# Block-sparse attention and MLP on one core: engine orders made anew, and three of four first summary spreads moved to GpSimd

## The chip, the cores and the metric

One Trainium2 chip, one of its cores. The metric is the device time of one execution in microseconds, the median of three runs, lower is better. Times in the profile count from the first instruction of the profiled execution.

## The reference

```python
def _attn_ref(q, k, v):                      # (4, 8, 768, 64) each, float32
    block, window = (32, 16)
    k_sum = k.reshape(B, H, nb, block, D).max(axis=3)
    v_sum = v.reshape(B, H, nb, block, D).mean(axis=3)
    scores_l = scale * np.matmul(q, k.transpose(0, 1, 3, 2))       # masked to |i - j| < 16
    scores_s = scale * np.einsum('bhsd,bhnd->bhsn', q, k_sum) + np.log(block)
    a = softmax(concat([scores_l masked, scores_s]))               # 768 + 24 columns
    return a @ concat([v, v_sum])

def _moe_ref(x, w_in, w_out):                # x: 3072 x 512, w_in: 512 x 2048, w_out: 2048 x 512
    h = x @ w_in
    g = h * erf(softplus(h))
    return g @ w_out
```

So every token attends to 31 neighbours and to 24 block summaries of its sequence (the maximum of 32 keys, the mean of 32 values), and the result goes through a two-layer MLP.

## The kernel before, in words

The 3072 tokens are cut into 6 chunks of 512. Attention is done by **quads**: a pair of heads (of 4 pairs) in one chunk, so 24 quads; quads 0 to 3 make chunk 0. A quad's scores (`scores`, L580) are matmuls of 64 queries by 96 neighbouring keys and by 24 key summaries. `softmax` (L617) takes the row maximum on VectorE (`red`), the exponentials on ScalarE (`exps`, eight per quad) and scales the rows by their sums on VectorE (`norm`). `transp` (L678) turns the probabilities on TensorE, ScalarE copies the two halves out of PSUM (`ptr`), `av` (L720) multiplies them with the values, and `xsplit` (L741) stores the result as a high and a low float32r part: the high part copied by ScalarE, the low part subtracted by VectorE (line 751). A float32 product is then three float32r matmuls. The MLP goes in 24 periods k = 0 to 23 (6 chunks by 4 groups of 512 hidden columns): `mm1` (L830) is the first layer, `mm2` (L1001) the second, with softplus and erf on ScalarE and the splitting of the hidden values on VectorE between them.

Weights come from HBM as 64-bit numbers. `convert` (L340) packs each of 16 units into float32 with three VectorE operations (L354, L357, L360), then ScalarE makes the high and VectorE the low part (L376). `w0` to `w3` below are the first four units; the products of quads 0 and 1 with group 0 need w0, those of quads 2 and 3 need w1.

The head of the program is special: quads 0 to 3 have their own loads (`load_qk_first`, `load_v_first`, `load_vw_first`). `ksum_first` (L523) makes a quad's key summaries with one VectorE maximum. `vsum_first` (L526) makes all value summaries with 12 slow float32 matmul passes, ScalarE copies them to SBUF (L534), and then each quad's 24 summary rows must be spread into rows 96 to 119 of that quad's value tile `vwf`, eight times side by side (24 x 1024 numbers): `rows_` (L536). Quad p's `av` waits for that (`vwg{p}`). In the kernel before ScalarE spreads three quads' rows and one quad's go by a DMA on SP.

Nothing is issued in the order of the code. Every operation is entered in a `Plan` (L59) with the engines that can do it and assumed durations; `Plan.order` (L104) then simulates the engines and takes, wherever one comes free, the ready operation with the smallest key. The key is a due time worked back from TensorE's order, plus an offset from the table `TUNE` (one entry per operation: offset, penalty for a change of ScalarE's table, which table, which engine). `first_dma` (L294) enters the first loads with assumed transfer times and an assumed landing. TensorE may take operations up to 60 ahead among the first 330, 8 ahead after that. Where the plan sees TensorE idle early, it puts filler matmuls (`busy`, L1047; line 1050 in the profile), at most one per 0.43 us of planned idle time.

Each DMA on SP also waits, in order, for the eighth before it to have landed; every engine executes its own list in order.

Of the kernel before, what the change touches and what calls it, by code (L numbers as in the profile page):

```python
# [23 lines left out]
NP = H // 2  # L24
# [3 lines left out]
NI = NB // 2  # L28
NT = T // 128
NS = 24  # L30
LW = 96
# [27 lines left out]
class Plan:  # L59
# [44 lines left out]
    def order(self, free, window, tune, table):  # L104
# [87 lines left out]
def block_attention_mlp(ctx: ExitStack, tc: tile.TileContext, q_t, k_nat, k_win, v_tok, v_nat, v_win, w_in, w_out, out):  # L192
# [101 lines left out]
    def first_dma(us, fn, r=(), w=(), **kw):  # L294
        return P.add({"SP": us}, lambda e: fn(), r, w, hold=2.0, land=-1.0, **kw)
# [31 lines left out]
    def load_w(u):  # L327
        kind, g, r = u
        n = raw_slot(u)

        def go():
            rw = raws[u] = slot(n, [128, 2, 512, 2], U32, "rw")
            src = (w_in[2 * g + r] if kind == "i" else w_out[2 * g + r]).bitcast(U32).rearrange("p c (f t) -> p c f t", t=2)
            nc.sync.dma_start(out=rw, in_=src)
        if u in units[:4]:
            first_dma(2.6, go, w=[f"w{n}"])
        else:
            dma(1112, go, w=[f"w{n}"])
# [169 lines left out]
    def load_qk_first(p):  # L508
        st[p] = dict(qb=qfs[:, p], vw=vws[p // 2][:, p % 2])
        first_dma(2.7 if p == 1 else 0.97, lambda: nc.sync.dma_start(out=kfirst[p], in_=k_nat[0, p]), w=[f"kf{p}"])  # L510
        first_dma(0.66, lambda: nc.sync.dma_start(out=qfs[:, p], in_=q_t[0, p]), w=[f"qf{p}"])

    def load_v_first():
        for n in range(2):
            def go(n=n):
                for t in range(3):
                    nc.sync.dma_start(out=vts[n][:, t], in_=v_tok[3 * n + t])
            first_dma(2.1 + 0.15 * n, go, w=[f"vt{n}"])

    def load_vw_first(p):  # L520
        first_dma(1.35, lambda: nc.sync.dma_start(out=st[p]["vw"], in_=v_win[0, p]), w=[f"vwf{p}"])
# [43 lines left out]
    def load_quad_v(qd):  # L565
# [12 lines left out]
    PA = ("pA", "pB")  # L578

    def scores(qd, banks=PA):  # L580

# [726 lines left out]
```

## Time and profile before

| | |
|---|---|
| time, median of 3 runs (lowest, highest) | 600.12 us (599.73, 600.18) |
| the profiled execution's own time | 599.8 us |
| its span, first to last instruction | 598.0 us |
| PE (TensorE) busy | 590.6 us, 99% |
| DVE (VectorE) busy | 476.4 us, 80% |
| ACT (ScalarE) busy, of it 98 table loads | 424.3 us, 125.7 us |
| POOL (GpSimd) busy | 4.0 us, all in the first 8 us |
| DMA moved | 169.93 MB, mean 284 GB/s |

Busy time counts an engine as busy also with filler matmuls, and a matmul's end is modelled, so 99% does not say that nothing is lost. The queue that issues DMAs is SP. In the profile PE is TensorE, DVE VectorE, ACT ScalarE, POOL GpSimd.

### The profile page before, as it was taken

The numbers are of one execution on the slowest core, as the hardware profiler recorded it, in microseconds if no ns is written. First come the engines' busy times: TensorE is split into PE (matmuls) and PEld (weight loads), VectorE is DVE, ScalarE is ACT, GpSimd is POOL, SyncE is SP. The second block draws the span as 40 slices with busy tenths as digits, with TensorE's granted clock in tenths as the row PEclk, the third lists the DMA queues.
The fourth block names the chain that finished last, engine by engine and source line by source line (L and its number), as shares of the span: only waits on it lengthen the run. The fifth ranks groups of instructions, "written<-read, shape, count | busy, mean of one in ns | idle before, by whom it ended". The sixth has DMA issues, their size and how long they took to land.

```text
span 598.0 us, 11682 instructions
## 1 busy us (share of the span) xinstructions
PE 590.6 (99%) x4495; PEld 486.1 (81%) x4495; DVE 476.4 (80%) x1001; ACT 424.3 (71%) x824; POOL 4.0 (1%) x30
## 2 busy tenths in 40 slices
PE   8899999999999999999999999999999999999997
PEld 4675666878888889989888888888888888888885
DVE  5999999888999987866989769669778677556553
ACT  6989879989879794674885964846646654852570
POOL 2000000000000000000000000000000000000000
PEclk9999999999999999999999999999999999999999
DMA  8999777668997989899998888787897864774621
GB/s 330 358 418 344 282 253 284 221 247 316 318 344 245 345 323 338 290 351 370 313 376 315 323 310 323 267 302 269 292 304 263 309 226 146 252 243 178 237 72 70
DMA packets 47586, 169.93 MB, mean 284 GB/s; under 512 B 4460, under 2 KB 16940, under 8 KB 34988
## 3 DMA queue, kind: packets, MB, share of 16 engines
q1 hardware_dynamic: 47388, 169.07, 78.1%
q8 instruction: 35, 0.57, 0.4%
q14 instruction: 19, 0.16, 0.1%
q10 hardware_dynamic: 144, 0.13, 0.1%
HBM read 135.66 MB, written 31.46 MB: 279 GB/s over the span
## 4 chain that ended last, share of the span: by engine, by line
PE 96%; ACT 1%; DVE 1%; issue 0%
PE ops L1013 41%; PE h L839 15%; PE ha L891 12%; PE hb L885 7%; PE ops L1009 5%; PE hb L891 4%; PE hb L882 4%; PE pA L600 3%; PE px L735 3%; PE px L732 1%; DVE stats L639 1%; PE pA L687 1%; PE idle L1050 1%; ACT prf L647 0%; PE pB L600 0%; ACT ptr L692 0%
## 5 line engine op out<-in xcount | busy, mean ns | idle before, releaser
L1013 PE MATMUL ops<-w,gh 128*128 128x512 f32 x704 | 230.1, 393 | 0.0
L1013 PEld LDWEIGHTS ops<-w,gh 128*128 128x128 f32 x704 | 132.3, 188 | 27.8 <-issue 0.9
L1013 PE MATMUL ops<-w,gl 128*128 128x512 f32 x352 | 137.5, 391 | 0.0
L1264 ACT ACT_TABLE_LOAD x98 | 125.7, 1283 | 1.7
L839 PE MATMUL h<-x,w 128*128 128x512 f32 x384 | 97.0, 402 | 0.0
L298 ACT COPY hc<-hb 128x256 f32<-128x256 f32 x65 | 23.9, 373 | 102.9 <-PE hb L882 57.0
L839 PEld LDWEIGHTS h<-x,w 128*128 128x128 f32 x384 | 71.1, 188 | 18.5 <-issue 3.6
L1013 PEld LDWEIGHTS ops<-w,gl 128*128 128x128 f32 x352 | 66.2, 188 | 11.8
L989 DVE TENSOR_TENSOR hc<-wt,hc 128x1024 f32<-128x1024 f32 x44 | 53.0, 1219 | 10.7 <-ACT wt L977 10.7
L647 ACT ACTIVATE prx<-prx,stats 128x120 f32<-128x120 f32 x160 | 61.0, 384 | 0.2
L996 DVE TENSOR_TENSOR gl<-hc,gh 128x1024 fp32r<-128x1024 f32 x44 | 53.6, 1220 | 1.0 <-ACT gh L298 0.2
L930 DVE TENSOR_TENSOR hc<-hb,hc 128x256 f32<-128x256 f32 x96 | 38.7, 418 | 15.8 <-ACT hc L298 14.6
L977 ACT ACTIVATE wt<-wt 128x1024 f32<-128x1024 f32 x48 | 50.1, 1058 | 0.4
L965 ACT ACTIVATE wt<-hc 128x1024 f32<-128x1024 f32 x32 | 33.0, 1055 | 8.2 <-DVE hc L930 8.0
L298 DVE CAST gh<-hc 128x1024 fp32r<-128x1024 f32 x37 | 25.5, 690 | 10.6 <-PE ops L1013 9.5
L885 PE MATMUL hb<-w,ws 128*128 128x512 f32 x96 | 30.2, 396 | 0.0
L647 ACT ACTIVATION_READ_ACCUMULATOR prx<-prx,stats 128x1 f32 x160 | 30.0, 187 | 0.0
L1009 PE MATMUL ops<-a32s,gw 128*128 128x512 f32 x64 | 29.6, 597 | 0.0
L633 DVE CUSTOM_DVE_ANT_0 prx<-pA,mask_sb 128x120 f32<-128x120 f32 x64 | 14.2, 278 | 17.7 <-PE pB L600 17.4
L298 DVE COPY hc<-hb 128x256 f32<-128x256 f32 x31 | 13.0, 418 | 18.0 <-PE hb L882 13.8
L891 PE MATMUL ha<-w,ws 128*128 128x256 f32 x192 | 27.2, 283 | 0.0
L891 PE MATMUL ha<-x,w 128*128 128x256 f32 x192 | 27.1, 282 | 0.0
(172 smaller groups left out, 959.8 us busy)
## 6 DMA issues: line engine op xcount, KB each, us to landing
w<-dr SPq DMA_DIRECT2D x36, 1024.0 KB
ws<-ds SPq DMA_DIRECT2D x30, 1024.0 KB
vw<-v_win SPq DMA_DIRECT2D x20, 512.0 KB
kw<-k_win SPq DMA_DIRECT2D x20, 480.0 KB
rw<-w_in SPq DMA_DIRECT2D x8, 1024.0 KB
rw<-w_out SPq DMA_DIRECT2D x8, 1024.0 KB
dr<-w SPq DMA_DIRECT2D x8, 1024.0 KB
dt<-ot SPq DMA_DIRECT2D x16, 512.0 KB
```

What stands on the lines that cost most here:

```text
L298: e.copy(o, i) if e is nc.scalar else e.tensor_copy(o, i)
L647: nc.scalar.activation(s["pr"][:, j], s["pr"][:, j] if qd >= MQ else s["sc"][j // NI][:, i * NK:(i + 1) * NK], AF.Exp, scale=-1.0 if qd >= ...
L839: nc.tensor.matmul(hs[k, f][:, 0:T], lhsT=w[m], rhs=xt[ch, cc][:, x], start=(cc == 0 and n == 0), stop=(cc == 3 and n == 2))
L885: nc.tensor.matmul(full, lhsT=w[0], rhs=y, start=first and c == 0, stop=c == 1, skip_group_check=True)
L891: nc.tensor.matmul(half, lhsT=w[m], rhs=y[:, l], start=first and c == 0 and i == 0, stop=c == 1 and i == 2, skip_group_check=True)
L930: on({"DVE": 0.43}, lambda e: e.tensor_tensor(hc[k, n][:, m, z], bank(n, "b")[:, R], hc[k, n][:, m, z], op=ALU.add), [pair_banks(n)[1]], [ ...
L977: act(0.96, lambda n=n: nc.scalar.activation(wt[k, n], wt[k, n], AF.Erf, scale=-1.0 if k < SOFT else 1.0), [s], [s], table=("sig",), after ...
L989: e.tensor_tensor(hc[k, n], wt.pop((k, n)), hc[k, n], op=ALU.mult)
L996: e.tensor_tensor(gs[k, n][1], hc.pop((k, n)), f32(gs[k, n][0]), op=ALU.subtract)
L1009: nc.tensor.matmul(os_[ch, t], lhsT=x[0][:, i % 2, t * 128:(t + 1) * 128], rhs=w32["o", g, i // 2][:, i % 2], start=first, stop=last)
L1013: nc.tensor.matmul(os_[ch, t], lhsT=x[y][:, i % 2, t * 128:(t + 1) * 128], rhs=w[m], start=first and n == 0, stop=last and n == 2)
L1264: nc.scalar.preload_act_table_set(sets[o["load"]])
```

## The change

`TUNE` is another table (one line of some 60,000 characters, of which only the start stands here), so the order on every engine is new from the first microseconds on. The assumed times of the first loads are changed, and eight of them get fixed places at the head of SP's list (`first`). The spreading of the summary rows may now be done by GpSimd, ScalarE or VectorE instead of ScalarE, VectorE or a DMA; the plan gives quad 0 to ScalarE and quads 1, 2 and 3 to GpSimd. Two further ways (`OWN`, `ASKED`) are in the code with empty lists, so nothing takes them.

```diff
-TUNE = {0: (-400.0, 1.5, 0, None), 1: (-300.0, 1.5, 0, None), 2: (-100.0, 1.5, 0, None), ...
+TUNE = {0: (1.06317, 1.5, 0, None), 1: (0.7965079, 1.5, 0, None), 2: (0.01488405, 1.5, 0, None), ...
...
-            key[n] = later + (n if "PE" in o["eng"] else o["due"])
+            key[n] = later + (n if "PE" in o["eng"] else o.get("first", o["due"]))
...
-        return P.add({"SP": us}, lambda e: fn(), r, w, hold=2.0, land=-1.0, **kw)
+        return P.add({"SP": us}, lambda e: fn(), r, w, hold=2.0, land=-0.9, **kw)
...
-        def summed():
-            nc.scalar.copy(vsum[LW:NK], tiles[bank][LW:NK].rearrange("s (p c) -> s p c", p=NP))
-        act(0.5, summed, [bank], [f"vsum0{p}" for p in range(NP)])
-        def rows_(e, p):
+        on({"ACT": 0.55, "DVE": 0.6}, lambda e: copy(e, vsum[LW:NK], tiles[bank][LW:NK].rearrange("s (p c) -> s p c", p=NP)), [bank], [f"vsum0{p}" for p in range(NP)])
+        def rows_(e, p, ask=False):
             o, i = st[p]["vw"][LW:NK], vsum[LW:NK, p:p + 1, :].to_broadcast([NS, NB, 128])
-            e.dma_start(out=o, in_=i) if e is nc.sync else copy(e, o, i)
+            e.dma_start(out=o, in_=i) if ask or e is nc.sync else copy(e, o, i)
         for p in range(NP):
-            on({"ACT": 0.95, "SP": 0.45} if p else {"DVE": 1.13, "ACT": 0.95}, lambda e, p=p: rows_(e, p), [f"vsum0{p}", f"vwf{p}"], [f"vwg{p}"])
+            ...
+                on(VWG, lambda e, p=p: rows_(e, p), [f"vsum0{p}", f"vwf{p}"], [f"vwg{p}"])
...
+    VWG = {"POOL": 1.6, "ACT": 0.95, "DVE": 1.13}
...
+    for n, p in enumerate((0, 1, 3, 2, 8, 4, 5, 9)):
+        P.ops[p]["first"] = n - 1e6
```

In total the instructions are the same but for these: 9 ScalarE table loads fewer (89 for 98 behind the first), one filler matmul fewer (12 for 13), the spreading as said (one copy on ScalarE for three, three on GpSimd for none, no DMA of `vsum` on SP), and some 10 small copies that go to the other of VectorE and ScalarE.

**VectorE, the first 10 us.** `kf_124` holds the keys of quads 0 and 1; `pA`, `pB` are the two halves of quad 0's scores, `h0`, `h1` those of quad 1. Before:

```order
L524 TENSOR_REDUCE ksum_112<-kf_124 128x24
L639 TENSOR_REDUCE stats_110<-pA_146 128x4
L641 TENSOR_SCALAR stats_110<-stats_110 128x4
L639 TENSOR_REDUCE stats_110<-pB_147 128x4
L641 TENSOR_SCALAR stats_110<-stats_110 128x4
L524 TENSOR_REDUCE ksum_112<-kf_124 128x24
L639 TENSOR_REDUCE stats_110<-h0_195 128x4
```

and now:

```order
L524 TENSOR_REDUCE ksum_112<-kf_124 128x24
L645 TENSOR_REDUCE stats_110<-pA_146 128x4
L647 TENSOR_SCALAR stats_110<-stats_110 128x4
L524 TENSOR_REDUCE ksum_112<-kf_124 128x24
L645 TENSOR_REDUCE stats_110<-pB_147 128x4
L647 TENSOR_SCALAR stats_110<-stats_110 128x4
L645 TENSOR_REDUCE stats_110<-h0_187 128x4
```

Quad 1's key summaries moved in between the two halves of quad 0's row maximum.

**ScalarE, from quad 1's exponentials to the turned probabilities of quad 1.** `ptr` are copies of turned probabilities (the first pair is quad 0's, the second quad 1's), `vsum<-vs` the value summaries, `vwf<-vsum` a spread, `w<-a32` the high part of w0, `x<-px` that of quad 0's attention output. Before:

```order
L647 ACTIVATE prf_130,stats_110<-o1_188,stats_110 128x120 x3
L692 COPY ptr_350<-pA_325 120x512
L692 COPY ptr_350<-pB_326 120x512
L534 COPY vsum_113<-vs_249 24x512
L298 COPY vwf_131<-vsum_113 24x1024
L298 CAST w_411<-a32_345 128x1024
L298 COPY vwf_131<-vsum_113 24x1024
L298 CAST x_436<-px_416 128x512
L692 COPY ptr_440<-pA_373 120x512
L692 COPY ptr_440<-pB_374 120x512
```

and now:

```order
L698 COPY ptr_325<-pA_305 120x512
L698 COPY ptr_325<-pB_306 120x512
L653 ACTIVATE prf_130,stats_110<-o0_218,stats_110 128x120
L653 ACTIVATE prf_130,stats_110<-o0_218,stats_110 128x120 x3
L653 ACTIVATE prf_130,stats_110<-o1_219,stats_110 128x120 x4
L298 COPY vsum_113<-vs_245 24x512
L298 COPY vwf_131<-vsum_113 24x1024
L298 CAST w_434<-a32_348 128x1024
L298 CAST x_437<-px_416 128x512
L698 COPY ptr_440<-pA_353 120x512
L698 COPY ptr_440<-pB_354 120x512
```

Quad 0's two copies moved ahead of quad 2's exponentials, and the second spread left ScalarE (it is the first of three that follow each other at the end of GpSimd's list).

**TensorE, the first products of the first layer.** `px` is an `av` (of quads 0 to 3 in turn), `x_436` and `x_437` quad 0's attention output, `x_508` and `x_503` quad 1's, `pA<-ident,prf` a matmul of a transposition. Before:

```order
L1050 MATMUL idle_133<-zeros_71 128x512
...
L732 MATMUL px_478<-ptr_440,vwf_131 64x64 x16
L839 MATMUL h_499<-x_436,w_411 128x512 x3
L839 MATMUL h_504<-x_436,w_411 128x512 x3
L839 MATMUL h_513<-x_436,w_411 128x512 x3
L839 MATMUL h_518<-x_436,w_411 128x512 x3
L839 MATMUL h_513<-x_508,w_411 128x512 x3
L732 MATMUL px_533<-ptr_510,vwf_132 64x64 x16
```

and now:

```order
L1061 MATMUL idle_133<-zeros_71 128x512
L743 MATMUL px_459<-ptr_440,vwf_131 64x64 x16
L850 MATMUL h_480<-x_437,w_434 128x512 x3
L693 MATMUL pA_485<-ident_65,prf_130 120x64
...
L850 MATMUL h_505<-x_437,w_434 128x512 x3
L850 MATMUL h_516<-x_437,w_434 128x512 x3
L850 MATMUL h_522<-x_437,w_434 128x512 x3
L850 MATMUL h_516<-x_503,w_434 128x512 x3
L743 MATMUL px_539<-ptr_512,vwf_132 64x64 x16
```

The transposition of quad 2, which stood before quad 1's `av` (behind the filler, in the place of the "..." of before), now stands behind the first three products.

## Rows read from the trace of the kernel before

**Rows 1.** The page: busy time by engine, and the chain that ended last by engine.

```profile
PE 590.6 (99%) x4495; PEld 486.1 (81%) x4495; DVE 476.4 (80%) x1001; ACT 424.3 (71%) x824; POOL 4.0 (1%) x30
...
PE 96%; ACT 1%; DVE 1%; issue 0%
```

**Rows 2.** Busy time by stretch; the second line names the columns.

```profile
core 0: us, PE busy (x) PEld busy (x) DVE busy (x) ACT busy (x) POOL busy (x), PEclk, DMA share, GB/s
...
15.00:20.00 5.00, 5.00 (x105) 3.15 (x103) 4.93 (x6) 4.95 (x20) 0.00 (x0) 1.00 1.04 412
...
42.00:100.00 58.00, 58.00 (x361) 36.40 (x360) 57.73 (x111) 51.98 (x102) 0.00 (x0) 1.00 0.84 306
100.00:300.00 200.00, 200.00 (x1558) 168.86 (x1557) 171.57 (x380) 159.75 (x302) 0.00 (x0) 1.00 0.86 307
```

**Rows 3.** What TensorE waited for: us in total, times, longest.

```profile
PE pA L687 <- ACT ptr L692: 1.3, 1, 1.3
...
PE px L732 <- ACT vwf L298: 0.4, 1, 0.4
```

**Rows 4.** TensorE in order of time: start, us, line, tiles, [idle before].

```profile
21.58 1.25 PE L1050 MATMUL idle<-zeros 128*128 128x512 bf16 x5
24.17 0.24 PE L687 MATMUL pA<-ident,prf 64*120 64x64 f32 x1 [1.34 <-ACT ptr L692]
...
24.88 1.15 PE L732 MATMUL px<-ptr,vwf 120*64 120x64 f32 x32
25.96 3.70 PE L839 MATMUL h<-x,w 128*128 128x512 f32 x15
...
37.73 0.39 PE L1050 MATMUL idle<-zeros 128*128 128x512 bf16 x1
...
37.77 4.46 PE L839 MATMUL h<-x,w 128*128 128x512 f32 x18
42.07 0.27 PE L485 MATMUL vt<-ident,vs_sum 128*128 128x128 f32 x1
```

**Rows 5.** VectorE in order of time.

```profile
7.42 0.65 DVE L639 TENSOR_REDUCE stats<-pB 128x4 f32<-128x480 f32 x1
...
8.19 0.94 DVE L524 TENSOR_REDUCE ksum<-kf 128x24 f32<-128x768 f32 x1
9.90 1.22 DVE L639 TENSOR_REDUCE stats<-h 128x4 f32<-128x480 f32 x2 [0.77 <-PE h L600]
...
22.88 1.15 DVE L657 TENSOR_TENSOR prf<-prf,stats 128x960 f32<-128x960 f32 x1
23.94 0.68 DVE L751 TENSOR_TENSOR x<-px,x 128x512 fp32r<-128x512 f32 x1
...
27.66 0.68 DVE L751 TENSOR_TENSOR x<-px,x 128x512 fp32r<-128x512 f32 x1
28.26 0.68 DVE L354 TENSOR_SCALAR a<-rw 128x1024 uint32<-128x1024 uint32 x1
```

**Rows 6.** ScalarE in order of time.

```profile
18.79 0.58 ACT L534 COPY vsum<-vs 24x512 f32<-24x512 f32 x1
19.40 1.04 ACT L298 COPY vwf<-vsum 24x1024 f32<-24x1024 f32 x1
...
21.53 1.04 ACT L298 COPY vwf<-vsum 24x1024 f32<-24x1024 f32 x1
22.60 0.58 ACT L298 CAST x<-px 128x512 fp32r<-128x512 f32 x1
...
23.56 0.60 ACT L692 COPY ptr<-pB 120x512 f32<-120x512 f32 x1
```

**Rows 7.** GpSimd in order of time.

```profile
2.46 0.26 POOL L233 TENSOR_SCALAR_AFFINE_SELECT band<-band 64x96 f32<-64x96 f32 x1
...
6.14 0.22 POOL L273 MEMSET pick<- 128x140 f32 x1
...
6.95 0.16 POOL L277 MEMSET prx<- 128x64 f32 x1
```

More of the change, by code (lines that the diff above doesn't have):

```diff
@@ L335, in load_w @@
         if u in units[:4]:
-            first_dma(2.6, go, w=[f"w{n}"])
+            first_dma(2.5, go, w=[f"w{n}"])
         else:
@@ L509, in load_qk_first @@
         st[p] = dict(qb=qfs[:, p], vw=vws[p // 2][:, p % 2])
-        first_dma(2.7 if p == 1 else 0.97, lambda: nc.sync.dma_start(out=kfirst[p], in_=k_nat[0, p]), w=[f"kf{p}"])
-        first_dma(0.66, lambda: nc.sync.dma_start(out=qfs[:, p], in_=q_t[0, p]), w=[f"qf{p}"])
+        first_dma((1.05, 1.0, 1.0, 1.0)[p], lambda: nc.sync.dma_start(out=kfirst[p], in_=k_nat[0, p]), w=[f"kf{p}"])
+        first_dma((0.65, 1.4, 0.65, 0.65)[p], lambda: nc.sync.dma_start(out=qfs[:, p], in_=q_t[0, p]), w=[f"qf{p}"])
     def load_v_first():
@@ L517, in go @@
                     nc.sync.dma_start(out=vts[n][:, t], in_=v_tok[3 * n + t])
[L518 removed]
+            first_dma(2.0 + 0.85 * n, go, w=[f"vt{n}"])
     def load_vw_first(p):
[L521 removed]
+        first_dma(1.28, lambda: nc.sync.dma_start(out=st[p]["vw"], in_=v_win[0, p]), w=[f"vwf{p}"])
     def ksum_first(p):
@@ L532, in vsum_first @@
             pe(0.87, lambda t=t: go(t), [f"vt{t // 3}"], [bank])
-        def summed():
-            nc.scalar.copy(vsum[LW:NK], tiles[bank][LW:NK].rearrange("s (p c) -> s p c", p=NP))
-        act(0.5, summed, [bank], [f"vsum0{p}" for p in range(NP)])
-        def rows_(e, p):
+        on({"ACT": 0.55, "DVE": 0.6}, lambda e: copy(e, vsum[LW:NK], tiles[bank][LW:NK].rearrange("s (p c) -> s p c", p=NP)), [bank], [f"vsum0{p}" for p in range(NP)])
+        def rows_(e, p, ask=False):
             o, i = st[p]["vw"][LW:NK], vsum[LW:NK, p:p + 1, :].to_broadcast([NS, NB, 128])
-            e.dma_start(out=o, in_=i) if e is nc.sync else copy(e, o, i)
+            e.dma_start(out=o, in_=i) if ask or e is nc.sync else copy(e, o, i)
         for p in range(NP):
-            on({"ACT": 0.95, "SP": 0.45} if p else {"DVE": 1.13, "ACT": 0.95}, lambda e, p=p: rows_(e, p), [f"vsum0{p}", f"vwf{p}"], [f"vwg{p}"])
+            if p in OWN:
+                P.last[f"vwg{p}"] = ()
+            elif p in ASKED:
+                act(0.4, lambda p=p: rows_(nc.scalar, p, True), [f"vsum0{p}", f"vwf{p}"], [f"vwq{p}"])
+                P.add({"POOL": 2.2}, lambda e: None, [f"vwq{p}"], [f"vwg{p}"])
+            else:
+                on(VWG, lambda e, p=p: rows_(e, p), [f"vsum0{p}", f"vwf{p}"], [f"vwg{p}"])
     def load_quad(qd):
@@ L578, in block_attention_mlp @@
     PA = ("pA", "pB")
+    OWN, ASKED = (), ()
+    VWG = {"POOL": 1.6, "ACT": 0.95, "DVE": 1.13}
     def scores(qd, banks=PA):
@@ L613, in scores @@
             pe(0.58, mask, ["mh"], banks, small=1)
-            pe(0.96, lambda: keys(near), [f"qf{qd}", f"kf{qd}"], banks, small=1)
-            pe(0.5, lambda: keys(lambda r, j: [(LW, ksum[r, 0, qd])]), [f"qf{qd}", f"ksum0{qd}"], banks, small=1)
+            pe(0.92, lambda: keys(near), [f"qf{qd}", f"kf{qd}"], banks, small=1)
+            pe(0.57, lambda: keys(lambda r, j: [(LW, ksum[r, 0, qd])]), [f"qf{qd}", f"ksum0{qd}"], banks, small=1)
     def softmax(qd, banks=PA):
@@ L725, in go @@
             xo = s["xo"] = ps("px", bank)
+            for a in range(2 if qd in OWN else 0):
+                r = slice(64 * a, 64 * a + 64)
+                rhs = s["pt"][LW:NK, :, 256 * a:256 * a + 256].rearrange("k x (n q) -> k n x q", n=NI)
+                nc.tensor.matmul(xo[r].rearrange("d (n x q) -> d n x q", n=NI, x=2), lhsT=vsum[LW:NK, qd, r], rhs=rhs, start=True, stop=False, skip_group_check=True)
             for j in range(NB):
@@ L731, in go @@
                         b = 64 * (NI * a + j // 2)
-                        nc.tensor.matmul(xo[r, o], lhsT=s["vw"][0:NK, j, r], rhs=s["pt"][0:NK, j % 2, b:b + 64], start=True, stop=True)
+                        nk = LW if qd in OWN else NK
+                        nc.tensor.matmul(xo[r, o], lhsT=s["vw"][0:nk, j, r], rhs=s["pt"][0:nk, j % 2, b:b + 64], start=qd not in OWN, stop=True, skip_group_check=qd in OWN)
                     else:
@@ L735, in go @@
                         nc.tensor.matmul(xo[r, o].rearrange("d (a q) -> d a q", a=2), lhsT=s["vw"][0:NK, j, r], rhs=s["pt"][0:NK, z:z + 2, NI * a + j // 2], start=True, stop=True)
-        pe(1.085, go, ["pt", "vw"] if qd >= NP else ["pt", f"vwf{qd}", f"vwg{qd}"], [bank], small=1)
+        pe(2.1 if qd in OWN else 1.15 if qd < NP else 1.085, go, ["pt", "vw"] if qd >= NP else ["pt", f"vwf{qd}", f"vsum0{qd}" if qd in OWN else f"vwg{qd}"], [bank], small=1)
     xt = {}
```

2 lines of the change are left out of this document (1 added, 1 removed).

## The prediction

> **What bounds the kernel now.** I read the page's busy times first, then the chain of waits, then busy time by stretch, then TensorE's own waits, and only then the first 42 us engine by engine. The page shows TensorE busy for 590.6 of 598.0 us, and 96% of the chain that ended last is TensorE's [rows 1]. A busy TensorE may still be running fillers, so the stretches matter more. From 42 us on it is busy in every one of them, 58.00 of 58 and 200.00 of 200 us [rows 2], and its list of waits has no row from there: the two kinds kept of that list, 1.3 us for a copy of turned probabilities and 0.4 us for a spread, both lie before 25 us [rows 3]. So behind 42 us time falls only with less TensorE work, and the change has the same matmuls there. What can be won is in the head. There TensorE runs five fillers from 21.58 and reaches its next real work at 24.17, starts the first product at 25.96, and runs one more filler at 37.73 [rows 4].
>
> VectorE is the engine behind it: 4.93 of 5 us between 15 and 20, and 57.73 of 58 us between 42 and 100 [rows 2]. Its last real pause is 0.77 us before 9.90 [rows 5].
>
> The profiled execution took 599.8 us (span 598.0), 0.3 under the median of 600.12. The sum is made on its rows; I take the difference off the median. A measurement of this kernel can tell about 0.2%, 1.2 us, from no change.
>
> **The change, part by part.**
>
> *Quad 1's key summaries between the halves.* Before, they start at 8.19, 0.77 us after the second half of quad 0's row maximum at 7.42 [rows 5]. TensorE's summary scores of quad 1 wait for them, and VectorE in turn waits 0.77 us for those scores. Moved ahead of the second half they start near 7.4, and the maximum that stood at 9.90 can start near 9.15. VectorE has no pause of that kind afterwards, so its list runs ahead by that much, less some 0.15 because sum and reciprocal of quad 0 now follow each other directly: I take **0.6**. The last jobs that the first products need were done at 24.62 (23.94 and 0.68, low part of quad 0's output [rows 5]). The same jobs in another order now end at 24.0, with w0's low part the last. The price is that ScalarE's second half of quad 0's exponentials starts some 0.3 later, which quad 1's, still later, hide.
>
> *One spread fewer in ScalarE's way.* ScalarE spreads at 19.40 and again at 21.53, then copies the high part at 22.60, and the second copy of quad 1's turned probabilities runs from 23.56 to 24.16 [rows 6]. The second spread is 1.07 (21.53 to 22.60). Ahead of it, w0's high part waits for VectorE's packing, so some 0.45 of VectorE's 0.6 arrives here. Together 1.5: the copies end near 22.65. The other removed spread, behind 25 us, was not on TensorE's path, and neither is the DMA of summary rows on SP. Quad 0's copies ahead of quad 2's exponentials fill a pause of ScalarE and cost nothing.
>
> *First product.* Before, 24.17 transposition of quad 2, 24.88 `av` of quad 1, 25.96 product [rows 4]: 1.8 behind the copies. Now the transposition stands behind the first three products, so only `av` is left, 1.08 (24.88 to 25.96) and 0.1 for the change: 22.65 + 1.2 = 23.85, which is **2.1** earlier. Only the third matmul there needs w0's low part of 24.0, so it barely waits. Off this go 0.7 for the transposition (24.17 to 24.88), done later now, and 0.2 for a new wait: quad 1's low part, before done at 28.34 (27.66 and 0.68 [rows 5]), is 0.6 earlier but has sum and reciprocal of quad 3 newly ahead of it (0.3), so 28.05. TensorE is there at 23.85 + 2.9 (twelve products, by 3.70 us for fifteen [rows 4]) + 0.8 = 27.55, and its second matmul of that group, 0.23 later, is the one that waits. The filler at 37.73 is no longer issued: 18 products took from 37.77 to 42.07, 4.3, of which 4.1 is work [rows 4]; with the wait around the filler I count 0.25. Quad 3's low part, for which it waited, now has one packing operation of w3 (1.1) behind it that was ahead of it.
>
> Sum: 2.1 - 0.7 - 0.2 + 0.25 = 1.45, taken as **1.4**.
>
> *GpSimd's three copies.* The trace has none of this kind. Nearest are a memset of 140 columns in 0.22 and one of 64 in 0.16, 0.8 ns a column, and an operation that reads and writes 96 columns in 0.26, 2.7 ns a column [rows 7]. For 1024 columns that is 0.9 to 2.8 us; I take 1.6, between them and near the memset's whole time over its columns. They begin when ScalarE has copied the summaries and the value tile has landed, near 19.2 by the bytes ahead of it, an estimate. Quad 1's is wanted at 22.65, 3.4 later, so even 2.8 is hidden; quad 2's at 28.5 and quad 3's at 32.5 leave more. Cost nothing; without that cover, a copy over 3.4 would delay the first product by its excess.
>
> One thing speaks against that. All GpSimd's work is over at 7.11 [rows 7], and VectorE's scaling of rows at 22.88 [rows 5], which reads two SBUF operands, has nothing of GpSimd beside it, so no row shows the two at once. The Trainium skill, SBUF — State Buffer, section "Who interferes with whom", says that such an instruction and a GpSimd one that reads SBUF exclude each other for their whole length. No run here shows it. By the rule the sum would lose its gain, as the second rival has it; without it, it stays at 1.4.
>
> *SP.* The fourth value tile and a load of values move ahead of w2, 0.9 MB, 2.2 us at the 412 GB/s of [rows 2]. VectorE asked for w2 at 28.26 [rows 5] and will at about 28.7; the 9.8 MB up to it take 24 us at that rate, from a start near 3, so 27 to 28. Just hidden, cost nothing; if late, VectorE stands still and the new lead shrinks one for one. Past SP's new places nothing else of the head has its landing at the edge.
>
> *Everything behind 42 us.* Nine ScalarE table loads less and other orders on all engines: no gain, since TensorE did not wait there. Changes between matmul kinds on TensorE are as many as before within two, at some 0.1 us each: nothing. The tail's order is the same.
>
> **Forecast.** 600.12 - 1.4 = **598.7**, if TensorE keeps its lead. Its own range is 598.2 to 599.3.
>
> **Rivals.**
>
> *VectorE takes the lead back, 599.5.* VectorE has 0.27 us of idle time in the 58 us behind 42 [rows 2], and its list is only 0.6 ahead while TensorE is 1.4 ahead. If a second-layer input or a late w2 is then the last thing TensorE waits for, only VectorE's 0.6 is left: 600.12 - 0.6 = 599.5, at worst 600.3. For it: that saturation. Against it: TensorE never waited for VectorE there, and along the new order VectorE has on the whole slightly less to do ahead of each split hidden block than before.
>
> *GpSimd and VectorE block each other, slower.* Place: 19 to 28 us, where VectorE has no slack. A copy in progress would hold up the scaling of quad 2's rows, the next one w0's low part, the third (its tile lands near 25.4) a packing operation of w1. With 1.6 us a copy and GpSimd first at each meeting I get 0.4 + 1.1 + 1.5 = 3.0 of delay for quad 1's low part; it is then done at 31.0, TensorE waits 2.9 longer, and the end is 598.7 + 2.9 = 601.6. It decides from a delay of 1.4 on; with VectorE first at each meeting, or copies of 0.9, the delay is 0.4 to 1 and the time stays under 600. With 2.8 a copy it would be near 603. For it: three copies in the fullest stretch of VectorE. Against: no row.
>
> *The change does not do what it says:* the new table could be made for landing times that do not come, and the head stay as it is: 600.1. I count it with the first rival.
>
> **How the numbers follow.** Forecast 0.5, VectorE takes the lead back 0.3, blocking 0.2. Faster by over 1.2 us (under 598.9): most of the forecast's range, 0.4, and 0.01 more from unseen savings. Slower by over 1.2 (over 601.3): about 0.6 of the blocking case and a little for a wait behind 42 us, 0.16. Within: 0.43. The range reaches from 598.0, half a microsecond beyond the forecast's better side, to 601.7.
>
> **What would show it.** Right: VectorE's maximum of quad 1 near 9.15, ScalarE's second copy of quad 1 done near 22.65, first product near 23.9, no pause of TensorE over 0.3 us behind it, GpSimd's copies under 2.8 us and VectorE's instructions beside them no longer than elsewhere. Wrong: a first product behind 24.5; VectorE's two-operand instructions in 19 to 28 us longer than 1.3, or starting late behind a GpSimd copy; a wait of TensorE for VectorE between 28 and 66.

## The result, and the profile after

The changed kernel takes **603.64 us** (median of six runs, 602.73 to 604.31), the kernel before 600.04 beside it: 1.0057 times as long, 95% interval 1.0044 to 1.007. Forecast were 598.7 and a range up to 601.7. The profiled execution has a span of 600.8 us, 2.8 more than before. In the comparisons further down 36 of the 161 runs of the kernel before, none of them profiled, took 601.2 to 605.4 us at the changed kernel's mean granted clock (0.993 to 0.997, the others 0.998 to 1.0), which widens the intervals there, and the one profile of the halves (`e_half`) is of a throttled execution of 833.59 us and is not used.

The page first, where the two groups of [rows 1] had 590.6 us and 96%:

```profile
PE 591.6 (98%) x4494; PEld 486.5 (81%) x4494; DVE 475.6 (79%) x998; ACT 408.8 (68%) x816; POOL 7.5 (1%) x33
...
PE 95%; DMA 3%; issue 1%; SPq 0%; ACT 0%; ACTq 0%
```

TensorE is busy 1.0 us longer, and the chain has 1% of "issue", time in which an engine waited for nothing that the profile shows. Busy time by stretch, with the stretches of [rows 2] and four short ones (x is a count of instructions, PEclk the granted clock):

```profile
core 0: us, PE busy (x) PEld busy (x) DVE busy (x) ACT busy (x) POOL busy (x), PEclk, DMA share, GB/s
...
15.00:20.00 5.00, 4.94 (x91) 2.83 (x89) 4.79 (x8) 4.58 (x20) 0.00 (x0) 1.00 1.04 412
42.00:100.00 58.00, 58.00 (x363) 36.48 (x362) 57.90 (x110) 53.47 (x100) 0.00 (x0) 1.00 0.77 269
...
22.00:24.00 2.00, 0.00 (x0) 0.00 (x0) 1.98 (x2) 0.00 (x0) 0.97 (x1) 1.00 0.98 381
24.00:26.00 2.00, 1.67 (x12) 0.90 (x13) 0.37 (x1) 0.98 (x3) 0.00 (x0) 0.63 1.07 437
26.00:28.00 2.00, 2.00 (x26) 1.27 (x26) 2.00 (x3) 2.00 (x11) 0.50 (x1) 0.51 0.99 412
28.00:30.00 2.00, 2.00 (x34) 1.45 (x31) 1.97 (x3) 1.81 (x9) 0.96 (x1) 1.00 1.02 426
```

Behind 42 us TensorE is as full as before. From 22 to 24 us it does nothing at all, and ScalarE nothing either. TensorE's own waits (us in total, times, longest) answer to [rows 3]:

```profile
PE px L743 <- issue: 2.9, 1, 2.9
PE idle L1061 <- DVE zeros L217: 1.1, 1, 1.1
PE h L606 <- DMA kf<-k_nat: 1.0, 1, 1.0
PE px L743 <- ACT vwf L298: 0.2, 1, 0.2
```

The wait for the turned probabilities, 1.3 us before, is gone. In its place stand 2.9 us for nothing visible. In order of time, TensorE, then ScalarE, answering to [rows 4] and [rows 6]:

```profile
20.52 0.91 PE L743 MATMUL px<-ptr,vwf 120*64 120x64 f32 x23 [0.16 <-ACT vwf L298]
24.33 0.65 PE L743 MATMUL px<-ptr,vwf 120*64 120x64 f32 x9 [2.90 <-issue]
...
26.73 1.69 PE L743 MATMUL px<-ptr,vwf 120*64 120x64 f32 x32
28.34 0.97 PE L850 MATMUL h<-x,w 128*128 128x512 f32 x3
...
50.26 3.17 PE L1020 MATMUL ops<-a32s,gw 128*128 128x512 f32 x7
```

```profile
19.42 1.04 ACT L298 COPY vwf<-vsum 24x1024 f32<-24x1024 f32 x1 [0.39 <-DMA vwf<-v_win]
...
25.02 0.59 ACT L298 CAST x<-px 128x512 fp32r<-128x512 f32 x1 [3.22 <-PE px L743]
...
25.98 0.60 ACT L698 COPY ptr<-pB 120x512 f32<-120x512 f32 x1
```

The product of quad 0's probabilities with its values (`av`) is 32 equal matmuls with nothing to wait for between them. TensorE issues 23, stands for 2.9 us, and issues the other 9. ScalarE needs the whole product for the high part and stands 3.22 us; everything of quad 1 follows. The first product of the MLP starts at 28.34 (before 25.96, forecast 23.85).

The last row of TensorE is the first product of the output. In both kernels exactly 72 products of the first layer lie ahead of it. It starts at 50.26, before at 47.37:

```profile
47.37 2.84 PE L1009 MATMUL ops<-a32s,gw 128*128 128x512 f32 x6
```

From there to the end are 550.54 us after and 550.63 before. So the whole loss between these two executions lies ahead of the 72nd product, 2.9 us, and the start of the output is the mark by which the runs below are compared.

VectorE and GpSimd, answering to [rows 5] and [rows 7]:

```profile
7.55 0.95 DVE L524 TENSOR_REDUCE ksum<-kf 128x24 f32<-128x768 f32 x1 [0.59 <-DMA kf<-k_nat]
...
9.79 1.22 DVE L645 TENSOR_REDUCE stats<-h 128x4 f32<-128x480 f32 x2 [0.52 <-PE h L606]
...
21.97 2.02 DVE L663 TENSOR_TENSOR prf<-prf,stats 128x960 f32<-128x960 f32 x1
...
27.38 0.69 DVE L354 TENSOR_SCALAR a<-rw 128x1024 uint32<-128x1024 uint32 x1
28.09 1.94 DVE L357 SCALAR_TENSOR_TENSOR a<-rw,a 128x1024 uint32<-128x1024 uint32 x1
```

```profile
20.77 2.20 POOL L298 COPY vwf<-vsum 24x1024 f32<-24x1024 f32 x2 [13.63 <-DMA vwf<-v_win]
27.50 1.46 POOL L298 COPY vwf<-vsum 24x1024 f32<-24x1024 f32 x1 [4.53 <-DMA vwf<-v_win]
```

Two instructions of VectorE that read two SBUF operands are long exactly beside GpSimd's copies: 2.02 us where the same scaling took 1.15 before [rows 5], and 1.94 where the same packing takes 1.22 elsewhere. There are then two suspects for the pause. One is GpSimd's first copy: it begins at 20.77, 0.44 us before the last matmul ahead of the pause. The other is in the rows of the DMA queues: the packets of instructions, of which one moves inside the pause. The queues' packets, MB and share of 16 engines, first from 12.5 to 21.8 us, where no packet of instructions is among them, then from 21.8 to 21.9:

```profile
q1 hardware_dynamic: 941, 3.84, 102.7%
...
q1 hardware_dynamic: 5, 0.04, 98.4%
q8 instruction: 1, 0.02, 63.8%
```

Queue q8 carries 35 packets of 16 KB in the whole run, in step with TensorE's instructions (9,103 records, so one packet for some 256). Its first begins at 11.33, the second at 21.83. In the kernel before they begin at 10.53 and 16.91; the second, in the stretch from 16.8 to 17.0:

```profile
q1 hardware_dynamic: 20, 0.07, 93.8%
q8 instruction: 1, 0.02, 32.2%
```

### The profile page after: what moved, and what is told of

It reads as the page before. It is cut to its first block, busy times and chain, and to the rows that moved or that the text cites. A ratio compares the mean times of both kernels' runs of the same rounds, so it can differ in the third digit from the quotient of the medians.

```text
span 600.8 us, 11681 instructions
## 1 busy us (share of the span) xinstructions
PE 591.6 (98%) x4494; PEld 486.5 (81%) x4494; DVE 475.6 (79%) x998; ACT 408.8 (68%) x816; POOL 7.5 (1%) x33
## 4 chain that ended last, share of the span: by engine, by line
PE 95%; DMA 3%; issue 1%; SPq 0%; ACT 0%; ACTq 0%
PE ops L1024 41%; PE h L850 15%; PE ha L902 11%; PE hb L896 7%; PE ops L1020 5%; PE hb L902 4%; PE hb L893 4%; PE pA L606 3%; PE px L746 3%; PE px L743 2%; DMA vwf<-v_win 1%; DMA kf<-k_nat 1%; PE pA L693 1%; PE pB L606 0%; PE idle L1061 0%
## 5 line engine op out<-in xcount | busy, mean ns | idle before, releaser
L298 DVE CAST gh<-hc 128x1024 fp32r<-128x1024 f32 x40 | 27.6, 690 | 8.4 <-PE ops L1024 8.0
L902 PE MATMUL ha<-x,ws 128*128 128x256 f32 x192 | 26.9, 283 | 0.0
L902 PEld LDWEIGHTS ha<-w,ws 128*128 128x128 f32 x192 | 25.0, 191 | 0.1
```

The costliest lines, as they stand in the source:

```text
L298: e.copy(o, i) if e is nc.scalar else e.tensor_copy(o, i)
L902: nc.tensor.matmul(half, lhsT=w[m], rhs=y[:, l], start=first and c == 0 and i == 0, stop=c == 1 and i == 2, skip_group_check=True)
```

## The experiments

**Theory A**: TensorE ran out of instructions. **Theory B**: GpSimd's copies stop it. In the expectations an instruction's number counts all of TensorE's records: the first 705 hold 347 matmuls, as many weight loads and 11 others, so that the 705th is the last ahead of the pause; the 449th lies 256 ahead of it.

### Who stops TensorE: four runs

The copies on another engine (`e_act`), and GpSimd's copies in the old order (`b_pool`):

```diff
-        o["fn"](o["on"])
+        o["fn"]("ACT" if o["w"] and o["w"][0].startswith("vwg") else o["on"])   # e_act, in the changed kernel
+        o["fn"]("POOL" if o["w"] and o["w"][0] in ("vwg1", "vwg2", "vwg3") else o["on"])   # b_pool, in the one before
```

> The changed order, with the three spreads on ScalarE in place of GpSimd; nothing else moves. Theory A (TensorE ran out of fetched instructions: its queue of instruction packets, q8, brought none between 11.33 and 21.83 us, and the pause of 21.43 to 24.33 us ends 1.5 us after that packet): the pause stays, 2 to 3.5 us in the middle of quad 0's product with the values, the first product of the MLP stays behind 27.5, the time is 602 to 604. Theory B (GpSimd's first copies, at 20.77, cause the pause): no pause over 0.5 us there, first product near 25.3, time 600 to 601. In either theory VectorE's normalisation of quad 2 falls from 2.02 back to 1.16 us and the packing of the second weight from 1.94 to 1.23, if GpSimd is what held them.

Measured: 605.12 us, 1.0077 [1.0049, 1.0104]. The pause is there with no GpSimd copy at all, after 23 matmuls, 2.95 us, and the packet begins at 21.42. **Theory B falls** as the cause of the pause. But the two long instructions are short again:

```profile
21.85 1.15 DVE L663 TENSOR_TENSOR prf<-prf,stats 128x960 f32<-128x960 f32 x1
...
28.04 1.23 DVE L357 SCALAR_TENSOR_TENSOR a<-rw,a 128x1024 uint32<-128x1024 uint32 x1
```

The expected time was missed by 1.1: three spreads on ScalarE cost 1.5 us more than on GpSimd (605.12 less 603.64).

> The order of before, with the spreads of quads 1, 2 and 3 on GpSimd (there ScalarE, a DMA of SyncE's queue, ScalarE). Theory A: TensorE's instruction packet near 16.9 us comes before the pause could begin, so no pause labelled issue over 0.5 us; SyncE's queue no longer stands from 13.9 to 24.1 us, so that the third packet comes later than 24.04 (26 to 31 us), still ahead of need near 32; time 599 to 601. Theory B: a pause of 2 to 3 us beside GpSimd's first copy, time 602 to 603. In either theory two-operand instructions of VectorE that lie beside a copy of GpSimd take 0.7 to 0.9 us longer each.

Measured: 601.55 us, 1.0018 [1.0001, 1.0034]; no pause, packet at 17.10, and two instructions of VectorE drawn out beside copies (the expected 599 to 601 was missed by 0.55):

```profile
24.49 1.04 POOL L298 COPY vwf<-vsum 24x1024 f32<-24x1024 f32 x1 [2.60 <-DMA vwf<-v_win]
30.75 1.36 POOL L298 COPY vwf<-vsum 24x1024 f32<-24x1024 f32 x1 [5.22 <-DMA vwf<-v_win]
```

```profile
24.90 1.18 DVE L354 TENSOR_SCALAR a<-rw 128x1024 uint32<-128x1024 uint32 x1
...
30.04 1.17 DVE L357 SCALAR_TENSOR_TENSOR a<-rw,a 128x1024 uint32<-128x1024 uint32 x1
31.13 2.06 DVE L376 TENSOR_TENSOR w<-a,w 128x1024 fp32r<-128x1024 f32 x1
```

The last of them, a weight step, takes 1.22 elsewhere, the copy alone 1.03; here they overlap and both are longer. The first, a packing step that reads only one SBUF operand, takes 0.69 elsewhere. The third packet came at 24.47, not at 26 or later: that part of the expectation was wrong.

Then SyncE's queue was held, so that fewer data were on their way (quad 2's spread goes to SyncE, whose queue then waits for the summary rows; in the second run two more loads stand behind it):

```diff
+        o["fn"]("SP" if o["w"] and o["w"][0] == "vwg2" else o["on"])   # e_hold, e_hold2
+    for n in (13, 110):                                                # e_hold2: quad 3's values, fourth value tile
+        plan.remove(at[n])
+        plan.insert(plan.index(at[53]) + 1, at[n])
```

> The changed order, with quad 2's spread as a DMA of SyncE's queue behind the load of quad 3's first values: the queue then waits for the summary rows and quad 2's values, so that the third weight and what follows are issued near 21 us and not from 17.40 on. Theory A, first form (the instruction packet was held up by transfers issued after it was due): the packet comes before 20 us, the pause shrinks below 1 us or goes, time 600 to 601.5. Theory A, second form (it was held up by what was already queued at 14 us): packet near 21.8 and pause 2 to 3.5 us as before, time 602 to 604. Theory B: the pause stays, GpSimd still copies near 20.8.

> As the run before, with the fourth value tile and quad 3's first values behind that DMA too: SyncE's queue issues nothing from about 13.3 to 20.5 us, as in before it issued nothing from 13.9 to 24.1. Theory A, first form: packet of instructions near 17 to 18 us, no pause, first product near 25.3 us, time 600 to 601. Theory A, second form: packet near 21.8, pause 2 to 3.5 us, 602 to 604. Theory B: the pause stays beside GpSimd's copy.

Measured: 603.65 us (1.0051 [1.0033, 1.0069]) and 603.72 (1.0053 [1.0036, 1.007]); packets at 21.64 and 21.50, pauses of 2.91 and 2.63 after 23 matmuls. What was issued after 13.4 us has no part in it. The first form of theory A falls, the second stands.

### Where it stops: six runs that shift the instructions

Only the warming matmuls at the very start are touched, which compute nothing:

```diff
-    busy(WARM)
+    for n in range(WARM):                      # e_half: 256 columns each, e_quarter: 128
+        for c in range(0, 512, 256):
+            nc.tensor.matmul(idle[:, c:c + 256], lhsT=zeros[:, 0:128], rhs=zeros[:, 0:256], start=True, stop=True)
```

`e_plus2` and `e_plus8` split one and four of the seven, each of which has 512 columns, into two of 256; the others take some away:

```diff
-    busy(WARM)
+    busy(WARM - 1)                             # e_plus2; e_plus8: WARM - 4, and eight halves
+    for n in range(2):
+        nc.tensor.matmul(idle[:, 256 * (n % 2):256 * (n % 2) + 256], lhsT=zeros[:, 0:128], rhs=zeros, start=True, stop=True)
```

```diff
-WARM = 7
+WARM = 6                                       # e_minus2; 3 in e_less and, in the kernel before, b_less
```

> The changed kernel, with each of the seven warming matmuls of 512 columns at the start split into two of 256: 14 instructions more on TensorE (7 weight loads, 7 matmuls), the same work and time, nothing else changed. Theory A with a place (TensorE asks for its next 16 KB of instructions at a fixed number of instructions, here about the 490th to 500th, and gets it soon where that falls among the long vsum matmuls of 14.5 to 17.8 us, but only when it has run dry where it falls among the short ones after 17.8): packet near 15 to 17.5 us, no pause over 0.5 us, first product near 25.4, time 600 to 601.5. If only the count at which it runs dry is fixed, and the packet is late whatever stands there: the pause moves ahead by 7 matmuls (after 16 of the 32 in place of 23), 2.5 to 3.5 us, time 603 to 604.5. Theory D (it is that product or its operands that pause): the pause stays after 23 matmuls.

> As the run before, with the warming matmuls in quarters: 42 instructions more ahead of everything. Theory A with a place: packet near 14 to 16 us, no pause, first product near 25.4, time 600 to 601.5. Fixed count with a late packet: the pause moves ahead by 21 matmuls, to the start of that product (2 of 32 done). Theory D: pause after 23 matmuls.

> The changed kernel with 3 warming matmuls in place of 7: 8 instructions fewer ahead of the rest. Theory A in either form: the pause stays and moves back by 4 matmuls, after 27 of the 32 in place of 23, length 2.5 to 3.3 us, time 602.5 to 604.5. Theory D: after 23.

> The kernel before with 3 warming matmuls in place of 7. Theory A with a place: there the packet came at 16.91 us with 489 instructions done, 4 before the vsum matmuls end; with 8 fewer ahead the asking falls behind them among the short ones, so the packet comes only when TensorE has run dry at the 705th instruction, within quad 0's product with the values (near 21.5 us), and the kernel before gets a pause of 2 to 3 us and 1.5 to 3.5 us on its time (601.5 to 603.5). Fixed count with transport delays of chance, or theory D: no change, 599.7 to 600.7.

Measured: halves 601.76 us (0.9999 [0.9976, 1.0022]), quarters 601.85 (1.0004 [0.9984, 1.0023]): **the pause at that place is gone and 1.8 to 1.9 us with it** (of halves this shows in `e_half_hold` below, which has them too). Against the kernel before that ran beside each, the loss falls from 3.6 to 1.1 and 1.2. With quarters the packet came at 16.36 and the first product at 25.57:

```profile
21.24 1.15 PE L743 MATMUL px<-ptr,vwf 120*64 120x64 f32 x32 [0.50 <-ACT vwf L298]
22.32 1.04 PE L1061 MATMUL idle<-zeros 128*128 128x512 bf16 x4
24.48 1.15 PE L743 MATMUL px<-ptr,vwf 120*64 120x64 f32 x32 [1.12 <-ACT prf L653]
25.57 0.96 PE L850 MATMUL h<-x,w 128*128 128x512 f32 x3
```

`e_less`, 603.27, and `b_less`, 600.56, were expected to pause and did not; their packets came at 19.58 and 17.76, and in `e_less` the whole head ran some 2 us late. So it is not the place of the asking among long or short matmuls that decides, and what the expectations call theory A with a place falls.

> The changed kernel with one of the seven warming matmuls split into two: 2 instructions more on TensorE. A1 (the asking for the next packet is missed only at this exact place in the stream): no pause, packet near 16 to 19 us, 600.9 to 602. A2 (it depends on when earlier transfers and packets came, and 14 or 42 more instructions moved that): the pause stays, one matmul earlier (after 22 of 32), 2.5 to 3.3 us, 602.7 to 604.3.

> Four of the seven split: 8 instructions more. A1: no pause, 600.9 to 602. A2: the pause stays, after 19 of the 32 matmuls, 602.7 to 604.3.

> One warming matmul fewer: 2 instructions less. A1: no pause, 600.9 to 602. A2: the pause stays, after 24 of 32, 602.7 to 604.3.

Measured: 603.78, 601.64 and 603.18 us. The stop moves matmul for matmul; two instructions more, eight more, two fewer, in this order:

```profile
20.89 0.91 PE L743 MATMUL px<-ptr,vwf 120*64 120x64 f32 x22 [0.16 <-ACT vwf L298]
24.69 0.90 PE L743 MATMUL px<-ptr,vwf 120*64 120x64 f32 x10 [2.89 <-issue]
```

```profile
20.66 0.80 PE L743 MATMUL px<-ptr,vwf 120*64 120x64 f32 x19 [0.16 <-ACT vwf L298]
22.36 0.62 PE L743 MATMUL px<-ptr,vwf 120*64 120x64 f32 x13 [0.90 <-issue]
```

```profile
21.18 0.92 PE L743 MATMUL px<-ptr,vwf 120*64 120x64 f32 x24 [0.16 <-ACT vwf L298]
24.99 0.45 PE L743 MATMUL px<-ptr,vwf 120*64 120x64 f32 x8 [2.90 <-issue]
```

With eight more the pause is 0.90, and the time is what the expectation gave for no pause. 22, 19 and 24 in place of 23: the stop stands at a count of instructions, not at a piece of work. The counts of whole stretches say the same, here from the start into the pause, of the changed kernel and of the one with two instructions more:

```profile
0.00:22.50 22.50, 19.10 (x347) 10.96 (x347) 16.10 (x32) 16.89 (x58) 5.59 (x32) 1.00 0.94 351
```

```profile
0.00:23.00 23.00, 19.29 (x347) 11.26 (x347) 16.22 (x32) 16.87 (x58) 5.72 (x32) 1.00 0.93 353
```

347 matmuls each. And TensorE goes on a fixed time after the packet has begun: 2.50 us in the changed kernel (21.83 to 24.33), 2.73, 2.60 and 2.42 in these three, whose packets began at 21.96, 19.76 and 22.57. With that, **theory A is shown**: TensorE has used up what it had fetched and waits for the next 16 KB.

The other packets show the same count, and when one is asked for. I set the start of each beside TensorE's records: in the changed kernel the 4th to the 35th begin while TensorE is between 36 records short of and 97 records past the end of a block of 256 (the 193rd record, the 449th, the 705th and so on), so with most of another block still in hand. The first three, where the DMA engines are full, begin 115, 256 and 135 records past such an end. The second is the one that came a whole block late.

### Why the packet is late

For each kernel I added up the bytes that the data queue had moved when the packet began, and looked which load they fall in, in the order of issue. In all six kernels with the long pause it is the 1 MB load of the second weight (issued at 12.46 to 13.89), 58 to 92% through; in all the others a load ahead of it. The queue moves some 412 GB/s throughout, so by itself this says little more than that the packet was late. Hence the next run, which takes that load out of the line (`for n in (13, 110, 15)` in the edit above):

> As the two runs that held SyncE's queue, but with the load of the second weight (1 MB, issued at 12.83 us in the changed kernel) held too: behind quad 2's values, issued at 11.84, the queue issues nothing until the summary rows are there (near 19.5). Reckoned by the bytes moved, the late packet of instructions was passed on in the middle of that 1 MB load in all six kernels that pause, and ahead of it in all eight that don't. Theory Q (a packet stands in one line with the data that were queued before it): with that load out of the line the packet comes near 17 to 19 us, no pause over 0.5 us, time 600.5 to 602. Theory N (the lateness has nothing to do with the line of data): packet near 21.5 again, pause 2.4 to 3 us, 602.5 to 604.5.

Measured: 603.94 us (1.0062 [1.0043, 1.0081]), the packet at 19.21, in the stretch from 19.2 to 19.3:

```profile
q1 hardware_dynamic: 9, 0.03, 73.9%
q8 instruction: 1, 0.02, 63.7%
```

```profile
20.46 0.91 PE L743 MATMUL px<-ptr,vwf 120*64 120x64 f32 x23 [0.17 <-ACT vwf L298]
21.88 0.50 PE L743 MATMUL px<-ptr,vwf 120*64 120x64 f32 x9 [0.50 <-issue]
```

2.3 us earlier than with the load in line (21.50 in `e_hold2`), about what 1 MB takes at 412 GB/s (2.5), and the pause shrinks from 2.63 to 0.50. When the packet began, all but 0.31 MB of the 7.86 MB queued by then had been begun in `e_hold2`, all but 0.18 of 6.82 in `e_hold3`. **Data already queued hold a packet of instructions up**, as far as one run can show it; the packet was 0.2 us later than theory Q allows. The time is no better, because the second weight now comes late: VectorE stands 2.88 us for it, and TensorE 2.61 us for VectorE at 31.75.

That a packet waits for all data queued before it is not shown. In the kernel before, 8.91 MB had been queued when TensorE came to its 449th record at 15.12, and the packet began at 16.91 with 5.71 MB begun: if it was asked for there, as the later packets suggest, it went ahead of the other 3.2. And six instructions more than in `e_plus2` moved the packet as far (21.96 to 19.76 in `e_plus8`) with no load touched. What decides how much of the queued data goes first stays open.

### What else is lost

Without the pause the changed order still needs 601.8, by the medians 1.1 to 1.7 more than before (600.62 beside it, 600.04 in the first comparison); the intervals of the two runs above do not tell it from before.

> The changed kernel with the seven warming matmuls in halves (which took the pause away) and the three spreads on ScalarE in place of GpSimd. If the copies on GpSimd cost what VectorE's lengthened instructions beside them show (1.4 to 1.6 us in the two), the run is 0.5 to 1.5 us faster than the one with halves alone (601.76): 600.3 to 601.3. If ScalarE's three spreads (1.04 each) and the wait of the third for its values cost as much on the other side: 601.5 to 602.5, as the run with the spreads alone on ScalarE was 1.5 slower than the changed kernel. In both, no pause over 0.5 us labelled issue.

> The changed kernel with the warming matmuls in halves (no pause) and quad 2's spread as a DMA of SyncE's queue (so GpSimd copies for quads 1 and 3 only). It tells what is left of the loss once the pause is gone. If GpSimd's copies beside VectorE's two-operand instructions make it: the normalisation of quad 2 stays at 1.15 and the first product comes earlier by up to 0.9 than with halves alone, 600.7 to 601.4 against 601.76. If the order itself makes it (quad 2's probabilities turned behind the first product, products that wait for VectorE): 601.4 to 602.2, no gain.

Measured: with the spreads on ScalarE 603.22 (1.0038 [1.0023, 1.0054]), again 1.5 slower than on GpSimd; with one of GpSimd's three copies given to a DMA **600.40** (0.9997 [0.998, 1.0015]), 1.36 faster than halves alone as the medians stand, 0.85 with each set against the kernel before that ran beside it (600.62 and 600.11). So the move to GpSimd is right against ScalarE, and that one copy cost about a microsecond. Which instruction of VectorE it held up in the halves is not shown: in `e_quarter` the scaling began first and was not lengthened, but the last step of w0 took 1.45 for 1.22 and a packing step beside the third copy 1.83 for 1.17. The run also holds SyncE's queue, as `e_hold` did; there, with the pause, the same edit brought nothing (603.65). What TensorE waited for in `e_half_hold`:

```profile
PE px L743 <- DVE x L762: 2.1, 2, 1.1
```

Four tries to beat both kernels: a second buffer for quad 1's turned probabilities in the old order, with quad 1's spread on GpSimd (`b_pt2`), and on top of `e_half_hold` VectorE's first long packing step of w2 behind quad 2's low part (`e_best1`), w2 loaded earlier too (`e_best2`), and `e_best1` with quarters for halves (`e_best3`).

```diff
-            s["pt"] = sb([NK, 2, T], F32, "ptr", "pt")
+            s["pt"] = sb([NK, 2, T], F32, "ptr", "ot" if qd == 1 else "pt")   # b_pt2, with ops 79 and 43 moved ahead, vwg1 on POOL
+    for n, m in ((114, 91),):                                                 # e_best1; e_best2 adds (53, 16)
+        plan.remove(at[n])
+        plan.insert(plan.index(at[m]) + 1, at[n])
```

> A version meant to beat both: the order of before, with a second buffer for quad 1's turned probabilities (so that ScalarE's copies of them need not wait for quad 0's product with the values and stand ahead of the first weight's cast), quad 1's spread on GpSimd, and quad 2's normalisation ahead of the first weight's last step on VectorE. If TensorE's wait of 21.58 to 24.17 us in before was for those copies alone: turning of quad 2 near 23.0, first product near 24.8 in place of 25.96, 72 products done near 46.3 in place of 47.37, time 598.8 to 599.6. If VectorE or the packet of instructions takes the lead: first product no earlier than 25.6, 600 to 602.

> A version meant to beat both: halves of the warming matmuls and quad 2's spread as a DMA, as in the run at 600.40, and on VectorE the first long packing instruction of the third weight behind quad 2's low part in place of ahead of w1's last step. In that run TensorE waited 1.13 us for quad 2's low part (done at 34.5, wanted at 33.65). If that wait is all that is lost there: low part near 33.2, the wait gone, 599.2 to 599.7. If VectorE as a whole bounds the stretch: the wait comes back at a later input, 600.0 to 600.6.

> As the run before, and the load of the third weight issued ahead of that DMA, so that VectorE no longer stands 1.17 us for it at 30.8. If VectorE bounds the stretch: 0.5 to 1.1 faster than the run before, 598.5 to 599.5; if not, the same as the run before.

> As the first of the two runs meant to beat both, with the warming matmuls in quarters in place of halves. With halves TensorE stood 0.7 to 1.5 us at its 449th instruction, 256 ahead of the 705th, until 2.4 us after the first packet had begun; with quarters the first packet had come at 9.57 us and no such stop was seen. If 256 instructions a packet hold: no stop over 0.3 us at either count, first product near 25 us, 599.0 to 599.9. If the packet is late here too: a stop at the 449th or 705th, 600.2 to 601.5.

Measured: 600.38 (1.0005 [0.9988, 1.0022]), 600.69 (0.9988 [0.997, 1.0005]), 601.34 (1.0004 [0.9984, 1.0024]) and 600.69 (0.9995 [0.998, 1.001]). **None can be told from before.** In `b_pt2` the turning of quad 2 started at 23.65 and the first product at 26.42, not near 23.0 and 24.8: TensorE's wait was not for those copies alone. In `e_best1` the wait of 1.13 was gone, but that execution's head was 1 us late, part of it here:

```profile
14.52 0.18 PE L606 MATMUL o<-ksum,qf 64*64 64x24 f32 x1 [1.53 <-issue]
```

This is a stop at the packet before, 221 matmuls in, 126 fewer than 347. The two stops stand at the 449th and the 705th record, exactly 256 apart: 221 matmuls, 222 weight loads and six others the one, 347, 347 and 11 the other. 16 KB over 256 are 64 bytes for each. With quarters (`e_best3`) no stop at either place showed, as expected, but TensorE waited 1.40 for ScalarE instead, and the first product came at 25.50, not near 25.

## Why the prediction was wrong

The step that failed is the first product at 23.85. It took for granted that TensorE has its instructions, and so worked from waits between engines alone. Point by point:

- **Bound: right.** From the first product of the output on, both kernels take the same within 0.1 us; TensorE has no wait behind 42 us, and all that changed lies in the head.
- **Key summaries between the halves, 0.6: nearly nothing.** The summaries did move, to 7.55 after 0.59 us of waiting for quad 1's keys, but the maximum of quad 1 started at 9.79, not 9.15. TensorE's other scores of quad 1 waited 1.0 us for the same keys and began at 7.66, as before (7.64); mask matmuls follow them in the new order, and the summary scores began at 9.08, before 9.19. The prediction looked at the summaries alone, and no row of it said when the keys come.
- **One spread fewer on ScalarE, copies done at 22.65: mis-sized even without the pause.** They end at 26.58 in the changed kernel; without the pause at 23.74 (`e_half_hold`) to 24.00 (`e_quarter`), before 24.16. The high part stands ahead of them and needs quad 0's product, which needs quad 0's spread, and that waited for its value tile, landed near 19.4 (in `e_quarter` its spread began at 20.15). Taking work off ScalarE behind that point brings 0.2 to 0.4, not 1.5.
- **First product 2.1 earlier: -2.4, it came later.** Without the pause 25.13 to 25.57, so 0.4 to 0.8 earlier. Of the pause's price, some 0.5 us is the clock: TensorE had stood since 21.43, and the granted clock in the stretches from 24 and from 26 us was 0.63 and 0.51, in the second near the lower of its two levels (1.2 GHz); `av` of quad 1 took 1.69 in place of 1.15. Four fillers took 1.89 where `e_quarter` has 1.04, but they fill a wait: `av` needs ScalarE's copies, which end at 26.58, and starts at 26.73. Without the pause `av` of quad 1 waits for VectorE too, which the prediction left out: in `e_half_hold` quad 0's low part ends at 23.78, the copies at 23.74, and TensorE, idle for 0.94, starts at 24.05.
- **Transposition later, 0.7: right** (some 0.6 in `e_quarter`). The wait for quad 1's low part, 0.2, was 0.55 there, behind GpSimd's last copy. The filler no longer issued, 0.25: right; 24 products with it took 5.84 before (36.23 to 42.07), 24 without it 5.58 (37.87 to 43.45).
- **GpSimd's copies, 1.6 each within 0.9 to 2.8: right in size** (1.03 alone, 1.46 beside VectorE), right that no one waits for them, and **wrong that they cost nothing**.
- **Second rival, blocking: right as a mechanism, too large, and not what decided.** Reckoned were 0.4, 1.1 and 1.5 us of delay; two meetings were seen, 0.87 (2.02 less 1.15) and 0.72 (1.94 less 1.22), with copies of 1.03 and not 1.6. Whichever starts second hardly runs until the first is over: the two end 1.02 and 1.07 us after the copy beside them, almost their whole time alone (1.15 and 1.22), and the copy that starts at 27.50, inside a packing step that ends at 28.07, ends 0.89 after it (alone 1.03). The rule of the Trainium skill, SBUF — State Buffer, section "Who interferes with whom", is borne out by these ends. The two SBUF operands that the prediction names are not the whole condition: the packing step of 1.18 in `b_pool`, 0.69 elsewhere, reads one. As much of the loss as that explains, 0.85 to 1.36 by `e_half_hold`, is the smaller part of 3.6.
- **First rival, VectorE takes the lead back: seen where the pause is gone.** TensorE's waits in `e_half_hold` are for VectorE, 2.1 us.
- **SP, w2 just hidden: right**; VectorE waits for no load between 26 and 50 us, nor, without the pause, in `e_quarter` between 20 and 50. Table loads and the body, no gain: right.

The signs named for "wrong" were the right ones, a first product behind 24.5 and two-operand instructions over 1.3. The cause of the larger part, the late packet, stood on no list, and 603.64 lies beyond every price that a rival was given. The spread of the changed kernel's runs, 1.6 us against 0.9, fits a pause whose end hangs on a queue, but that was only argued.

## What to carry to other kernels

Before reckoning a gain of a microsecond or two in a head where DMA is saturated, look for TensorE's packets of instructions in the queue rows and count 256 of its instructions, weight loads too, from one to the next: in this head many short matmuls use up 256 in 6 to 7 us, and the packet was up to 7.8 us on its way. A stop labelled "issue" in the middle of like matmuls with no wait between them is the sign; splitting idle matmuls ahead of it, or moving the large load, tests it in one run. In these runs a GpSimd copy was free beside VectorE's reductions, and where it began first it cost 0.2 to 0.9 us beside an instruction with two SBUF operands (1.45 for 1.22 to 2.02 for 1.15) and 0.5 beside a packing step with one.

## What the runs showed of the hardware that I had not expected

TensorE stopped behind its 347th matmul in eight kernels (it ended at 21.17 to 22.09 us), and behind the 221st in four kernels with halves, until 2.4 to 2.7 us after a 16 KB packet had begun. The Trainium skill, Runtime: NRT & Kernel Launch, section "Instruction fetch mechanics", has the block size, 16 KiB or 256 instructions, with which the distance of the two stops agrees; it calls the cost of crossing a block "mostly hidden", and here it was 2.9 us and a clock at half speed for 3.4 us behind it (24.53 to 27.94). The packet was up to 7.8 us on its way, reckoned from the 449th record (13.99 us), the end of the block before, to its start at 21.83.

That eight instructions more for the same warming work, ahead of everything, make a kernel of 600 us faster by 2 us (603.64 to 601.64), while two more or two fewer do nothing (603.78, 603.18), is the plainest form of it. Whether the kernel before stops in this way in executions other than the profiled one, no trace shows.
